# Retention on 64x64 TensorE tiles from batch 2 on, with compact states and paired query loads

## The chip, the cores and the metric

One core of a Trainium2 chip runs the whole program. The metric is the device time in microseconds (us); the times are medians of several executions. Engines: PE is TensorE, DVE VectorE, ACT ScalarE, POOL GpSimd, SP SyncE, which here mainly issues DMAs.

## The reference

Eight batches of eight heads, 576 positions, head size 64. Retention without softmax, then a two-layer perceptron with GELU over all 4608 tokens:

```python
scores = scale * np.matmul(q, k.transpose(0, 1, 3, 2))      # q, k, v: (8, 8, 576, 64)
Dmat = np.where(rel >= 0, gamma[h] ** rel, 0.0)              # rel = i - j, one gamma for each head
attn = np.matmul(scores * Dmat, v)                           # (8, 8, 576, 64)
x = attn.transpose(0, 2, 1, 3).reshape(4608, 512)
h = x @ w_in                                                 # 512 -> 2048
out = gelu_tanh(h) @ w_out                                   # 2048 -> 512, float32
```

## The kernel before

**Chunks.** Each batch is four chunks `c` of 128 positions and a tail of 64. Inside a chunk the product is computed directly and masked; what lies before it comes through a running state of 64x64 for each head. The decay is folded into scale factors that are multiplied onto q and k when they are cast to fp16 (`cast`), so that masks hold only ones and zeros. Heads go in four pairs `p`; `hl` is the head in its pair. A chunk takes, on PE:

- `score`: keys times queries, 64 rows by 128 columns of the array, for each head 128 columns, into two banks `st`, which DVE multiplies by the causal mask `cm` into `ret` (`masks`);
- `past`: the state before the chunk times the queries, on the whole array, with the two states of a pair on the diagonal of a 128x128 block (`tbd`, zeros elsewhere; `tbt` holds the state for the tail);
- `av`: `ret` times values, 128 rows by 64 columns, added into the same bank `xs`;
- `state`: keys times values, added to the running state by `scan` (DVE) and copied into `tbd` by `spread` (ACT, two copies of 64 partitions each).

`put` (ACT) copies `xs` into `xT`, the perceptron's transposed input. The tails of two batches go together (`load_tails`, `cast_tails`, then `score`, `past`, `av` and `put` with a batch number from 100 on). Batches 0 and 1 (`b < NPE`) use another form already: two tokens on a partition, and 64x64 tiles of the array (`score2`, `state2`, `av2`).

**Loads.** `pump` issues the loads on SP in the order of `seq`, as the 16 buffers `ld` come free: batch 0, `w_in` in 16 blocks of 128 rows, `w_out`, batch 1, then the others. A load of a later batch takes 128 positions of all heads, in packets of 256 bytes. Keys and queries are then transposed by two DMAs (`turn_dma`, also on SP).

**Perceptron.** Nine blocks `t` of 512 tokens. In a block, 16 steps of `up` (128x512 products with `w_in`, GELU on ACT into `gT`, sums on DVE by `act_sums`) are followed by 14 half products `prod` with `w_out`; both layers save products by sums of submatrices. The last two blocks (`WIN`) use that for the first layer too.

**Order.** It is written out by hand. `at(t, u, f)` places `f` behind step `u` of block `t`; PE, ACT, DVE and POOL take their instructions in this order. Retention of batch `t + 1` lies in block `t`: scores of chunks 0 and 1 at `s0` (step 9 or 11), their outputs at `o0` (15) with the scores of chunks 2 and 3, whose outputs are at `o1` (24); the tails of `TP` had their scores at `s0` and their outputs at `o0`. In block 1 the steps are 21, 23, 25 and 28. Casts of batch `t + 2` stand at steps 16 to 23 and its transposes behind them.

**Banks.** All eight PSUM banks are handed out by `bank` in the order in which `drop` gave them back, so a new use of a bank waits for its last reader.

Of the kernel before, what the change touches and what calls it, by code (L numbers as in the profile page):

```python
# [20 lines left out]
def kernel(  # L21
# [27 lines left out]
    NT4 = 4  # L49
# [41 lines left out]
    def load(b, key, c):  # L91
        src = SRC[key]
        t = lds()
        if b < NPE:
            g, y = c // 2, c % 2
            nc.sync.dma_start(  # L96
                out=t.rearrange("p (n x) -> p n x", n=4),
                in_=src[b, y::2, 256 * g : 256 * g + 256, :].rearrange("n (p j) d -> p n (j d)", j=2),
            )
        else:  # L100
            nc.sync.dma_start(  # L101
                out=t.rearrange("p (h d) -> p h d", d=D),
                in_=src[b, :, 128 * c : 128 * c + 128, :].rearrange("h s d -> s h d"),
            )
        att[b]["raw"][key, c] = t
# [3 lines left out]
    def load_w_in(g, ct):  # L109
        t = lds()  # L110
        nc.sync.dma_start(out=t, in_=moe_w_in[128 * ct : 128 * ct + 128, 512 * g : 512 * g + 512])
        w_raw["i", g, ct] = t
# [50 lines left out]
    ip = const.tile([128, 4], I32, name="ip")  # L163
    nc.gpsimd.iota(ip[:, 0:2], pattern=[[1, 2]], base=-64, channel_multiplier=2)
    nc.gpsimd.iota(ip[:, 2:4], pattern=[[0, 2]], base=-64, channel_multiplier=1)
# [3 lines left out]
    ps5 = const.tile([128, 8], F32, name="ps5")  # L169
    nc.vector.tensor_copy(out=ps5[:, 0:4], in_=ip)  # L170
    for s, m in ((slice(0, 2), 128.0), (slice(3, 4), 64.0)):
        nc.vector.tensor_scalar(out=ps5[64:128, s], in0=ps5[64:128, s], scalar1=m, scalar2=None, op0=ALU.subtract)
    nc.vector.tensor_scalar(out=ps5[:, 4:8], in0=ps5[:, 0:4], scalar1=-1.0, scalar2=None, op0=ALU.mult)
    lp = const.tile([128, 64], F32, name="lp")
    sc = const.tile([128, 64], F32, name="sc")

    def pairs(x, n):
        return x[:, 16 * n : 16 * n + 16].rearrange("p (n j l) -> p n j l", j=2, l=2)

    lg = lgr.rearrange("p (n l) -> p n l", l=2).unsqueeze(2).to_broadcast([128, 4, 2, 2])  # L180
    for n in range(2):
        pj = ps5[:, 4 * n : 4 * n + 2].unsqueeze(1).unsqueeze(3).to_broadcast([128, 4, 2, 2])
        nc.vector.tensor_tensor(out=pairs(lp, n), in0=lg, in1=pj, op=ALU.mult)
        nc.vector.tensor_tensor(
            out=lp[:, 32 + 16 * n : 48 + 16 * n].rearrange("p (x h) -> p x h", h=8),
            in0=ps5[:, 4 * n + 2 : 4 * n + 4].unsqueeze(2).to_broadcast([128, 2, 8]),
            in1=lgr.unsqueeze(1).to_broadcast([128, 2, 8]), op=ALU.mult,
        )
    lq = lp.rearrange("p (g n x) -> p g n x", g=2, n=2)[:, :, 0]
    nc.vector.tensor_scalar(out=lq, in0=lq, scalar1=math.log(scale), scalar2=None, op0=ALU.add)  # L190
    nc.scalar.activation(out=sc, in_=lp, func=AF.Exp)
    sp = {key: sc[:, 16 * n : 16 * n + 16].rearrange("p (n l) -> p n l", l=2) for n, key in enumerate("qk")}
    sc = sc[:, 32:64].rearrange("p (s h) -> p s h", h=8)
# [7 lines left out]
    cm = const.tile([128, 128], F32, name="cm")  # L201
    tm = const.tile([128, 128], F32, name="tm")
# [11 lines left out]
    def chunk_masks():  # L214
        for m in (cm, tm):
            nc.gpsimd.memset(m, 1.0)
            nc.gpsimd.affine_select(
                out=m, in_=m, compare_op=ALU.is_ge, fill=0.0, base=0, pattern=[[1, 128]], channel_multiplier=-1
            )
        nc.gpsimd.memset(tm[0:64, 64:128], 0.0)  # L220
# [5 lines left out]

    tbt = [const.tile([128, HP, 128], F16, name=f"tbt{i}") for i in range(NT4)]

# [27 lines left out]
    def cast(b, key, c, eng):  # L256
# [8 lines left out]
        elif b < NPE:  # L265
# [7 lines left out]
        else:  # L273
            s0 = {"q": 0, "k": 2}[key] + (b >= PAIR)
# [3 lines left out]
                in1=sc[:, s0].unsqueeze(2).to_broadcast([128, 8, D]),  # L278
# [36 lines left out]

    def tq(b, c, p):
        return att[b]["tt"][:, 1, 8 * (c // 2) + 2 * p + c % 2 if b < NPE else 4 * c + p, :]
# [49 lines left out]
    def av2(b, g):  # L367
        a = att[b]
        for p in range(HP):
            for j in range(2):  # L370
                o = 256 * (p % 2) + 128 * j
                for h, hl in TILES:
                    nc.tensor.matmul(
                        a["xs", 2 * g + h][hv(hl), 128 * p : 128 * p + 128],
# [4 lines left out]
    def score(b, c):  # L379
        st = [bank("st") for _ in range(2)]  # L380
        for p in range(HP):
            for hl in range(2):
                nc.tensor.matmul(  # L383
                    st[hl][:, 128 * p : 128 * p + 128], att[b]["tt"][hv(hl), 0, 4 * c + p, :],
                    tq(b, c, p)[hv(hl)], start=True, stop=True,
                )
        att[b]["st", c] = st

    def masks(b, c):
        for hl, t in enumerate(att[b].pop(("st", c))):  # L390
            r = sb.tile([128, 512], F16, tag="ret", name="ret", bufs=6)
            nc.vector.tensor_tensor(  # L392
                out=r.rearrange("p (n i) -> p n i", i=128), in0=t.rearrange("p (n i) -> p n i", i=128),
                in1=(cm if b < PAIR else tm).unsqueeze(1).to_broadcast([128, 4, 128]), op=ALU.mult,
            )
            drop(t)
            att[b]["ret"][c, hl] = r
# [4 lines left out]
    def state(b, *cs):  # L402
        a = att[b]
        us = bank("us")
        for n, c in enumerate(cs):
            for p in range(HP):
                for hl in range(2):
                    nc.tensor.matmul(
                        us[64 * hl : 64 * hl + 64, 256 * n + 64 * p : 256 * n + 64 * p + 64],
                        a["k"][:, col(c, p, hl)],  # L410
                        a["v"][:, col(c, p, hl)],
                        start=True, stop=True,
                    )
            a["U", c] = (us, n, n == len(cs) - 1)
# [15 lines left out]
    def spread(b, c, cp):  # L430
        w = att[b].pop(("w", c))
        for hl in range(2):
            r = slice(64 * hl, 64 * hl + 64)
            cp(out=(tbd[b % 2][r, c, :, r] if c < NC - 1 else tbt[b % NT4][r, :, r]), in_=w[r])  # L434

    def past(b, c):
        xs = bank("xs")
        att[b]["xs", c] = xs
        if b >= PAIR:
            for n in range(2):  # L440
                for p in range(HP):
                    o = 64 * n
                    nc.tensor.matmul(
                        xs[:, 128 * p + o : 128 * p + o + 64], tbt[(b - PAIR + n) % NT4][:, p, :],
                        tq(b, 0, p)[:, o : o + 64],
                        start=(n == p == 0), stop=True, skip_group_check=True,
                    )
        elif c > 0:
# [6 lines left out]
    def av(b, c):  # L455
        a = att[b]
        for p in range(HP):
            for hl in range(2):
                nc.tensor.matmul(  # L459
                    a["xs", c][64 * hl : 64 * hl + 64, 128 * p : 128 * p + 128],  # L460
                    a["v"][:, col(c, p, hl)],
                    a["ret"][c, hl][:, 128 * p : 128 * p + 128],
                    start=(b < PAIR and c == 0 and p == 0), stop=True, skip_group_check=True,
                )
# [207 lines left out]
    def after(t, m, u):  # L672
# [7 lines left out]
        def send(o, i):  # L680
            if t < B:
# [107 lines left out]
    nc.vector.memset(tbt[0], 0.0)  # L789
# [25 lines left out]
    past(0, 0), past(0, 1)  # L815
# [17 lines left out]
    past(0, 2), past(0, 3)  # L833
# [24 lines left out]
    at(0, -12, lambda: [V.memset(x, 0.0) for x in (tbd[1][:, 1:], *tbt[1:])])  # L858
# [7 lines left out]
    def group(b, g, turns, s, o, own=True, ahead=(), apart=0, late=None):  # L866
# [19 lines left out]
        def second():  # L886
            past(b, 2 * g), past(b, 2 * g + 1), av2(b, g)
# [30 lines left out]
    def scores(t, c, tails=None):  # L918
        b = t + 1
        if b < B:  # L920
            score(b, c), score(b, c + 1)
        if tails is not None:
            score(PAIR + tails, 0)
        if b < B:
            masks(b, c), masks(b, c + 1)
        if tails is not None:
            masks(PAIR + tails, 0)

    def outs(t, c, tails=None, ahead=None):
        b = t + 1  # L930
        work = [(b, c), (b, c + 1)] if b < B else []
# [153 lines left out]
```

## Time and profile before

| | |
|---|---|
| median of three runs | 293.28 us (292.59 to 293.52) |
| profiled execution | 293.76 us, its span 292.0 us |
| granted TensorE clock | 0.996 |
| PE, DVE, ACT, POOL busy | 280.1, 204.1, 169.8, 100.0 us |
| DMA | 139585 packets, 53.95 MB; 118048 of them under 512 bytes |

A timeline line gives the start in the span, the time from the first start to the last end, engine, source line, operation, result and operands, array shape, tile and type, and the count. Matmuls overlap in their pipeline, so a group's time is longer than what it adds to the stream; the step from one group's start to the next one's is what counts.

### The profile page before, as it was taken

To read this page: it belongs to the slowest core of one execution; us is meant where nothing else is said; L and a number is where in the kernel's file an instruction comes from. 1 tells how busy PE (TensorE), PEld (TensorE's weight loads), DVE (VectorE), ACT (ScalarE), POOL (GpSimd) and SP (SyncE) were. 2 spreads that over 40 slices of the span, in tenths; PEclk is the share of its full clock that TensorE was granted. 3 is DMA by queue.
4 is the path that set the end of the run, shared out by engine and by line. 5 is a ranking of instruction groups with operands and counts; after the bars stand their busy time and mean duration, and the time that the engine had idled before them with its cause. 6 is when DMAs were issued, how large, how long until landed. Compare 5 with 4: busy or idle time off the path is not lost.

```text
span 292.0 us, 7383 instructions
## 1 busy us (share of the span) xinstructions
PE 280.1 (96%) x3024; PEld 207.6 (71%) x3024; DVE 204.1 (70%) x409; ACT 169.8 (58%) x321; POOL 100.0 (34%) x128
## 2 busy tenths in 40 slices
PE   6889998999999999999999999999999999999993
PEld 2558877888874687468845884488548887887783
DVE  7796998666864874477548834784489968974863
ACT  5487754987249545964396647664666258507810
POOL 4589779910661175008500730068030000000000
PEclk9999999999999999999999999999999999999998
DMA  6999999989999999999999979997952030003013
GB/s 195 308 382 370 364 293 228 252 213 163 225 192 230 235 206 183 244 235 210 200 267 209 218 147 270 216 190 99 271 95 38 2 144 3 0 21 125 3 36 108
DMA packets 139585, 53.95 MB, mean 185 GB/s; under 512 B 118048, under 2 KB 131360, under 8 KB 139552
## 3 DMA queue, kind: packets, MB, share of 16 engines
q1 hardware_dynamic: 138960, 52.97, 80.4%
q8 instruction: 23, 0.38, 0.6%
q10 hardware_dynamic: 592, 0.52, 0.5%
q14 instruction: 10, 0.08, 0.1%
HBM read 36.70 MB, written 9.44 MB: 158 GB/s over the span
## 4 chain that ended last, share of the span: by engine, by line
PE 66%; SPq 8%; DMA 8%; ACT 5%; POOL 5%; DVE 5%; issue 1%; POOLq 0%; DVEq 0%; ACTq 0%
PE hp L480 18%; PE opB L665 11%; PE opA L665 8%; PE opC L665 7%; SPq L101 5%; DMA ld<-in_moe_w_in_dram 4%; PE hp L501 4%; PE hB L574 3%; SPq L96 3%; ACT gT L486 3%; PE xs L459 2%; POOL w_out_sb L771 2%; PE st L383 2%; DMA ld<-in_v_dram 2%; DMA ld<-in_q_dram 2%; PE hC L574 2%
## 5 line engine op out<-in xcount | busy, mean ns | idle before, releaser
L480 PE MATMUL hp<-xT,w_in_sb 128*128 128x512 f16 x352 | 79.1, 379 | 0.6 <-ACT xT L469 0.3
L486 ACT ACTIVATE gT<-hp 128x512 f16<-128x512 f32 x88 | 50.1, 600 | 22.6 <-PE hp L480 22.0
L480 PEld LDWEIGHTS <-w_in_sb 128*128 128x128 f16 x352 | 34.0, 98 | 39.0 <-issue 1.1
L665 PEld LDWEIGHTS <-gT 128*128 128x128 f16 x576 | 54.9, 98 | 8.9 <-issue 0.9
L665 PEld LDWEIGHTS <-s 128*128 128x128 f16 x432 | 42.2, 98 | 4.9
L642 DVE TENSOR_TENSOR s<-gT 128x512 f16<-128x512 f16 x36 | 15.6, 434 | 31.2 <-ACT gT L486 24.5
L665 PE MATMUL opA<-w_out_sb,gT 128*128 128x256 f16 x288 | 36.0, 273 | 0.6 <-ACT w_out_sb L771 0.4
L392 DVE TENSOR_TENSOR ret<-st,cm 128x512 f16<-128x512 f32 x48 | 30.2, 681 | 3.6 <-PE st L383 3.6
L469 ACT CAST xT<-xs 128x512 f16<-128x512 f32 x36 | 19.2, 590 | 20.4 <-PE xs L459 17.0
L501 PE MATMUL hp<-xT,w_in_sb 128*128 128x256 f16 x256 | 29.9, 273 | 0.9 <-POOL w_in_sb L771 0.5
L275 POOL TENSOR_TENSOR ck<-ld,sc 128x512 f16<-128x512 f32 x24 | 25.0, 1043 | 9.7 <-DMA ld<-in_k_dram 9.7
L501 PEld LDWEIGHTS <-w_in_sb 128*128 128x128 f16 x256 | 24.3, 98 | 5.2 <-POOL w_in_sb L771 2.3
L434 ACT CAST tbd<-ws 64x256 f16<-64x256 f32 x48 | 19.4, 403 | 14.8 <-DVE ws L425 14.2
L275 POOL TENSOR_TENSOR cq<-ld,sc 128x512 f16<-128x512 f32 x24 | 26.1, 1088 | 2.6 <-DMA ld<-in_q_dram 2.1
L665 PE MATMUL opB<-wt,gT 128*128 128x256 f16 x224 | 26.8, 273 | 0.0
L979 POOL COPY gate<-s 128x1 f16<-128x1 f16 x5 | 0.9, 190 | 74.6 <-DVE s L646 74.6
L262 ACT CAST cv<-ld 128x512 f16<-128x512 f32 x24 | 14.2, 618 | 17.2 <-DMA ld<-in_v_dram 17.1
L508 ACT ACTIVATE gT<-hp 128x512 f16<-128x512 f32 x32 | 18.3, 605 | 3.5 <-PE hp L501 3.3
L679 DVE TENSOR_TENSOR k<-k,opB 128x512 f32<-128x512 f32 x17 | 11.7, 686 | 11.7 <-PE opB L665 10.7
L644 DVE TENSOR_TENSOR gT<-gT 128x512 f16<-128x512 f16 x36 | 18.0, 499 | 0.0
L665 PE MATMUL opB<-wt,s 128*128 128x256 f16 x144 | 17.4, 273 | 0.0
L665 PE MATMUL opC<-wt,s 128*128 128x256 f16 x144 | 17.2, 272 | 0.0
(122 smaller groups left out, 406.4 us busy)
## 6 DMA issues: line engine op xcount, KB each, us to landing
ld<-in_q_dram SPq DMA_DIRECT2D x32, 256.0 KB, 5.2
ld<-in_k_dram SPq DMA_DIRECT2D x32, 256.0 KB, 5.1
ld<-in_v_dram SPq DMA_DIRECT2D x32, 256.0 KB, 5.3
out_dram<-ost SPq DMA_DIRECT2D x16, 512.0 KB, 3.9
ld<-in_moe_w_in_dram SPq DMA_DIRECT2D x16, 256.0 KB, 5.7
ld<-in_moe_w_out_dram SPq DMA_DIRECT2D x16, 256.0 KB, 5.6
lt<-in_k_dram SPq DMA_DIRECT2D x8, 128.0 KB, 4.7
lt<-in_q_dram SPq DMA_DIRECT2D x8, 128.0 KB, 4.4
```

Of the source, the lines that this page charges most:

```text
L101: nc.sync.dma_start(out=t.rearrange("p (h d) -> p h d", d=D), in_=src[b, :, 128 * c : 128 * c + 128, :].rearrange("h s d -> s h d"),)
L275: eng.tensor_tensor(out=dst.rearrange("p (h d) -> p h d", d=D), in0=raw.rearrange("p (h d) -> p h d", d=D), in1=sc[:, s0].unsqueeze(2).to_ ...
L392: nc.vector.tensor_tensor(out=r.rearrange("p (n i) -> p n i", i=128), in0=t.rearrange("p (n i) -> p n i", i=128), in1=(cm if b < PAIR else ...
L434: cp(out=(tbd[b % 2][r, c, :, r] if c < NC - 1 else tbt[b % NT4][r, :, r]), in_=w[r])
L469: nc.scalar.copy(out=xT[:, g0 : g0 + 2], in_=xs.rearrange("p (n g t) -> p g n t", n=HP, g=2))
L480: nc.tensor.matmul(hp.rearrange("p (g t) -> p g t", t=TL), w_in_sb[:, ct, 128 * fc : 128 * fc + 128], xT[:, o : o + TB // TL, ct, :], star ...
L486: nc.scalar.activation(out=gT[t][:, fc].rearrange("p i n -> p (i n)"), in_=hp, func=AF.Gelu_apprx_tanh)
L501: nc.tensor.matmul(hps[n][:, 256 * x : 256 * x + 256].rearrange("p (g t) -> p g t", t=TL), w_in_sb[:, ct, 128 * (fs[n] + x) : 128 * (fs[n] ...
L508: nc.scalar.activation(out=gT[t][:, f : f + 2, 2 * u : 2 * u + 2, :].rearrange("p f i n -> p f (i n)"), in_=hp.rearrange("p (f n) -> p f n ...
L642: nc.vector.tensor_tensor(out=s["1"], in0=a21, in1=a22, op=ALU.add)
L644: nc.vector.tensor_tensor(out=a21, in0=a11, in1=a21, op=ALU.subtract)
L665: nc.tensor.matmul(op[tag][:, HD * u : HD * u + HD], lhs(f), rhs[:, f], start=(new and f == 0), stop=(f == NH - 1), skip_group_check=True,)
```

## The change

From batch 2 on and for all tails, every retention product but the first state of batch 2 uses 64x64 tiles: a product of 128 rows is split into two of 64.

- *Scores and values:* the quarter of each 128x128 product that the mask makes zero is left out. One piece has 128 columns, the other 64. Masks cover 384 columns of a bank in place of 512.
- *States* are kept without the zeros of the blocks (`tbc`, `tbt` of 64 columns), one ACT copy each.
- *Queries* are loaded with two tokens on a partition, in packets of 512 bytes, as in batches 0 and 1. Odd chunks of keys and values are loaded in two halves, upper rows first.
- *Output halves:* the heads of odd pairs lie in exchanged halves of `xT` (`hl ^ p % 2`), so odd row blocks of `w_in` are loaded as two exchanged halves. Output rows of blocks 2 to 7 are stored by two DMAs each.
- *Row tiles in turns:* `pack` takes all products of a place together and deals them to the four tiles by columns used so far. In a phase each row tile writes other banks than the other; between phases a matmul of 4 columns into a bank of its own (`TURN`) is issued.
- *Order:* scores of chunks 2 and 3 are packed with the outputs of chunks 0 and 1; tail outputs move from `o0` to `o1`, the third `later` to step 21, the last value cast of batches 4 to 7 from step 23 to 25; block 4 has `s0` at 11.

```diff
-        if b < NPE:
+        if b < NPE or key == "q":
...
+        else:
+            for n in range(2):
+                r0 = 128 * c + 64 - 64 * n
+                nc.sync.dma_start(
+                    out=t[64 * n : 64 * n + 64].rearrange("p (h d) -> p h d", d=D),
+                    in_=src[b, :, r0 : r0 + 64, :].rearrange("h s d -> s h d"),
+                )
...
-        nc.sync.dma_start(out=t, in_=moe_w_in[128 * ct : 128 * ct + 128, 512 * g : 512 * g + 512])
+        for r, n in ((slice(0, 128), 0),) if ct % 2 == 0 else ((slice(0, 64), 64), (slice(64, 128), -64)):
+            rows = slice(128 * ct + r.start + n, 128 * ct + r.stop + n)
+            nc.sync.dma_start(out=t[r], in_=moe_w_in[rows, 512 * g : 512 * g + 512])
...
-    cm = const.tile([128, 128], F32, name="cm")
-    tm = const.tile([128, 128], F32, name="tm")
+    cm = const.tile([128, 192], F32, name="cm")
+    tm = const.tile([128, 64], F32, name="tm")
...
+        two = lambda n: [[1, 2], [2, n // 2]]
+        causal(cm, 128, 0, 64, 64, two(64)), causal(cm, 128, 64, 128, 64, two(128))
+        causal(cm, 64, 0, 128, 0, two(128)), causal(cm, 64, 128, 64, 0, two(64))
+        causal(tm, 128, 0, 64, 64, [[1, 64]]), causal(tm, 64, 0, 64, 0, [[1, 64]])
...
+    def pack(*phases, n=None):
+        opened = set()
+        for phase in phases:
+            if not phase:
+                t = ps.tile([128, 512], F32, tag=f"p{n}", name="turn", bufs=1)
+                nc.tensor.matmul(t[0:64, 0:4], ident[0:64, 0:64], ident[0:64, 0:4], start=True, stop=True)
+                continue
+            todo = {x: deque() for x in TILES}
+            for r, jobs in phase:
+                for x, *job in jobs:
+                    if r in (x[0], None):
+                        todo[x].append(job)
+            free = dict.fromkeys(TILES, 0)
+            while any(todo.values()):
+                x = min((x for x in TILES if todo[x]), key=lambda x: free[x])
+                t, out, lhsT, rhs, cols = todo[x].popleft()
+                k = (id(t), x[1])
+                nc.tensor.matmul(out, lhsT, rhs, start=k not in opened, stop=True, skip_group_check=True)
+                opened.add(k)
+                free[x] += cols
+        if n is not None:
+            spare.append(n)
+
+    TURN = ()
+
+    def piece(o, first):
+        w = 128 if first else 64
+        return o if first else 1 - o, w, 0 if o == 0 else 64 if first else 128
+
+    def score(b, g, x, first=(0, 1)):
...
+        return [
+            ((r, h), st[r], by_two(st[r][hv(h), i + 192 * (p % 2) : i + 192 * (p % 2) + w]),
+             a["tt"][hv(r), 0, 4 * (2 * g + o) + p, hv(h)], tq2(b, 2 * g + o, p, r, w), w)
+            for p in (2 * x, 2 * x + 1) for first in (True, False) for o in range(2)
+            for h, w, i in [piece(o, first)] for r in range(2)
+        ]
...
+        if b >= NPE or c == NC - 1:
+            cp(out=tbt[b % NT4] if c == NC - 1 else tbc[b % 2][:, c], in_=w)
+            return
...
+    def outs(b, g, tails=None, ahead=None, more=False):
+        n = spare.popleft()
+        x, y = outputs(b, g)
+        if more:
+            u, = state(*ahead)
+            s, z = score(b, 1, 0), score(b, 1, 1, (1, 0))
+            pack(
+                [(0, x), (1, y), (0, u), (1, s[:8])], TURN, [(None, s[8:]), (0, s[:8]), (1, z)], TURN,
+                [(0, y), (1, x), (0, z), (1, u)], n=n,
+            )
+        elif tails is not None:
+            t, = outputs_tails(PAIR + tails, 1)
+            if ahead is not None:
+                u, = state(*ahead)
+                pack([(0, t), (1, u)], TURN, [(0, x), (1, y)], TURN, [(0, u), (1, t)], TURN, [(0, y), (1, x)], n=n)
+            else:
+                pack([(1, t)], [(0, x), (1, y)], TURN, TURN, [(0, y), (1, x), (0, t)], n=n)
+        elif ahead is not None:
+            u, v = state(*ahead)
+            pack([(0, u), (1, v)], TURN, [(0, x), (1, y)], TURN, [(0, v), (1, u)], TURN, [(0, y), (1, x)], n=n)
+        else:
+            pack([(0, x), (1, y)], TURN, TURN, [(0, y), (1, x)], n=n)
+        put(b, 2 * g), put(b, 2 * g + 1)
+        if tails is not None:
+            put_tails(PAIR + tails)
...
-        s0, o0, s1, o1 = U2 if t == 1 else (11 if t in (2, 3) else 9, 15, 15, 24)
+        s0, o0, s1, o1 = U2 if t == 1 else (11 if t in (2, 3, 4) else 9, 15, 15, 24)
...
-        t0, ut, go = b - 2, [16, 16, 17, 18, 18, 19, 20, 20, 21, 22, 22, 23], 29
+        t0, ut, go = b - 2, [16, 16, 17, 18, 18, 19, 20, 20, 21, 22, 22, 25], 29
```

In `piece`, `o` is the chunk in its pair of chunks, `first` the piece of 128 columns. In the lists of `outs`, `(0, x)` means the products of list `x` on row tile 0.

## The prediction

> **What bounds the kernel now.** The page comes first: part 1 (busy time) and the PE and DMA rows of part 2 (40 slices of 7.3 us).
>
> ```profile
> PE 280.1 (96%) x3024; PEld 207.6 (71%) x3024; DVE 204.1 (70%) x409; ACT 169.8 (58%) x321; POOL 100.0 (34%) x128
> ...
> PE   6889998999999999999999999999999999999993
> ...
> DMA  6999999989999999999999979997952030003013
> ```
>
> TensorE (PE) works 280 of 292 us, and from the fifth slice on it hardly pauses; no other engine passes 70%. So what the change takes out of PE's own stream counts nearly one for one, unless something else becomes late. The DMA row is full until about 200 us, so loads are the first suspect for being late. The PE timeline of block t=2 shows what retention costs there:
>
> ```profile
> 94.88 0.62 PE L383 MATMUL st<-tt 64*128 64x128 f16 x16
> 95.44 3.63 PE L480 MATMUL hp<-xT,w_in_sb 128*128 128x512 f16 x16
> 98.90 0.39 PE L450 MATMUL xs<-tt,tbd 128*128 128x128 f16 x4
> 99.22 0.64 PE L459 MATMUL xs<-ret,cv 128*64 128x128 f16 x16
> 99.69 0.42 PE L408 MATMUL us<-cv,ck 128*64 128x64 f16 x16
> 100.04 0.62 PE L383 MATMUL st<-tt 64*128 64x128 f16 x16
> 100.59 1.92 PE L665 MATMUL opA<-w_out_sb,gT 128*128 128x256 f16 x16
> ...
> 108.46 0.61 PE L450 MATMUL xs<-tt,tbd 128*128 128x128 f16 x8
> 109.00 0.64 PE L459 MATMUL xs<-ret,cv 128*64 128x128 f16 x16
> 109.47 0.42 PE L408 MATMUL us<-cv,ck 128*64 128x64 f16 x16
> 109.82 1.05 PE L665 MATMUL opA<-w_out_sb,gT 128*128 128x256 f16 x8
> ```
>
> Read start against next start. Sixteen score matmuls (L383) lie between dense work for 0.56 us; the block at 98.90 takes 1.69 us, the one at 108.46 1.36 us. In the recorded starts, a pair of two half-array products is 56 ns apart from the next pair at 128 columns and 28 to 32 ns at 64. Each change of array shape costs 93 to 100 ns over that. Four 64x64 tiles at once occur only in batches 0 and 1:
>
> ```profile
> 53.92 0.45 PE L359 MATMUL us<-cv,ck 64*64 64x64 f16 x32
> 54.20 0.62 PE L332 MATMUL st<-tt 64*64 64x128 f16 x32
> 54.75 2.81 PE L501 MATMUL hp<-xT,w_in_sb 128*128 128x256 f16 x24
> ```
>
> 32 of 64 columns take 0.28 us and 32 of 128 take 0.55 us with the way out. The four of a quartet start 3 to 4 ns apart; quartets follow after 32.2 ns (64 columns) or 55.6 ns (128). These are the prices of everything the change adds. The whole block costs 0.91 us against dense work on both sides, and 8 x 32.2 + 8 x 55.6 ns is 0.70, so entering and leaving costs 0.2 us.
>
> **PE, before.** I take each retention block from batch 2 on as the next dense start, less the previous dense start and that matmul's 109 or 216 ns. By block: t=1 0.64 + 1.29 + 0.64 + 1.35; t=2 0.64 + 1.68 + 1.35; t=3 and t=4 (with tails) 0.86 + 2.14 + 1.35 each; t=5 as t=2; t=6 0.86 + 2.14 + 1.10; t=7 0.42 + 0.66. Sum 25.1 us.
>
> **PE, after.** The built program has 21 blocks on 64x64 tiles with 528 matmuls of 128 columns and 928 of 64: 132 x 55.6 + 232 x 32.2 ns = 14.8 us. Scores and values fall by a quarter of their columns, past states by half, state products keep theirs. Phases that end in a turn wait for the fullest of the four tiles; walking the built order with these spacings adds 1.4 us. The 32 turns (64x64, 4 columns) have no row. From below they cost 4 ns, the gap inside a quartet; from above a shape change, 95 ns. I take 32 ns, the nearest row (the 64-column quartet: weights of the same size must load for each), in all 0.9 us. The Trainium skill, TensorEngine Tiling (Array Packing), Instruction Overhead, gives a short matmul about 60 cycles; at the 2.4 GHz that its page TensorE: Matmul & The Clock Gate gives, an estimate is 25 ns a turn and 0.7 us in all, and no run here shows it.
>
> Entering and leaving is 21 x 0.2 = 4.2 us. In the built order each later turn of a block also waits for the turn before it, whose result takes about as long as a 64-column matmul, 193 ns. Where 16 short matmuls lie between (four times) some 90 ns stay uncovered, where two turns follow each other (twice) some 200 ns: 0.75 us. Sum 14.8 + 1.4 + 0.9 + 4.2 + 0.75 = 22.1 us, so PE gains 3.0 us. With turns of 4 ns and those waits free it is 4.6 us, with turns of 95 ns 1.1 us.
>
> **Waits on PE.** At t=1, step 23, the two state banks are the last two score banks. DVE drains four masks in 2.48 us (74.04 to 76.5); at three quarters of the columns I take 0.53 each, to 76.1, while PE comes to them near 75.8. What is queued behind is all of PE: +0.3 us. At the later blocks the banks are older by four dense steps (3.5 us). Against this, one wait should go:
>
> ```profile
> 113.06 0.62 ACT L262 CAST cv<-ld 128x512 f16<-128x512 f32 x1 [3.63 <-DMA ld<-in_v_dram]
> ...
> 114.70 10.52 PE L480 MATMUL hp<-xT,w_in_sb 128*128 128x512 f16 x48 [0.34 <-ACT xT L469]
> ```
>
> ACT sits in a cast that waits for a load, the output copy (`put`) is behind it, and PE idles 0.34 us. The last value cast moves from step 23 to 25, behind that copy: -0.3 us.
>
> **DVE, ACT, POOL.** Masks shrink from 512 to 384 columns, and the 64 half-height state copies (`spread`, 403 ns each) become 38; with ACT at 58% and DVE at 70% this is worth nothing on the path. Two half copies for the last tails cost some 0.4 us of an ACT that waits then. `chunk_masks` has four more selects on POOL (0.3 us each, less the removed memset): about +1.0 us ahead of batch 2's casts. Its cover is a wait:
>
> ```profile
> 60.01 1.13 POOL L275 TENSOR_TENSOR cq<-ld,sc 128x512 f16<-128x512 f32 x1 [1.91 <-DMA ld<-in_q_dram]
> ```
>
> If this cover went, the 1.0 us would reach the transposes. Start-up constants gain one DVE operation and lose memsets: 0, bounds 0.2 us either way.
>
> **Loads and stores.** A 256-byte packet took 22.2 ns on average, one of 512 bytes 30.6. A load of 256 KB is then 1.42 or 0.98 us of 16 engines; 24 query loads save 10.6 us of a DMA system that is busy 80% of 292. Each odd key or value load becomes two halves: SP issues of the halved tail loads took 0.63 us each, whole ones at least 0.57, query loads of 512 bytes 0.37. So a batch's issues go from 12 x 0.6 to 4 x 0.38 + 4 x 0.6 + 8 x 0.63, 7.2 to 9.0 us. They now leave SP over 15.6 us (93.18 to 108.77), at the pace of the DMA, so this hides. Output stores of blocks 2 to 7 are cut in two: 2 x 0.4 us on SP ahead of the next loads, hidden the same way. The eight extra `w_in` issues fall where loads leave every 0.7 us for 0.33 us of issue; fewer bytes are then in flight, 0 to 0.5 us, I take 0.2. The tails' products move from step 15 to 24; at t=6 the transpose on SP that waits for them (7.8 us now) waits some 10 us more, with only stores behind it that come later still and its reader at 244.
>
> The narrowest place is the transposed batch:
>
> ```profile
> L308 SPq DMA_TRANSPOSE tt<-cq x1: 3251/3251/3251, 67.5 to 67.5; - x1
> ...
> DMA to landing us min/median/max: 5.6/7.0/8.4
> ```
>
> The query transpose issued at 67.47 landed 5.6 us later, at 73.1; PE reads it at 73.54. For t=2 the slack is 93.9 to 94.88; from t=3 on 3 us and more.
>
> **Sum.** -3.0 + 0.3 - 0.3 + 0.2 = -2.8 us. The profiled execution took 293.76 us (span 292.0, 1.7 around it), the median 293.28. From the median: 290.5 us.
>
> **Rivals.**
> *Turns are dear (slower).* If a turn drains the array, the next phase starts only when the last result is written: 216 ns, the length of one 128-column matmul. 14.8 + 1.4 + 4.2 + 32 x 0.216 = 27.3 us, 2.2 more than before, 295.7 with the rest. It decides from about 140 ns a turn on. For it: a turn exists to keep two row tiles out of one bank, and some turns do wait for another. Against it: most wait only for a turn long past, and even a shape change costs 95 ns. Chance 0.10.
>
> *Issue limit (slower).* Batches 0 and 1 never run more than 64 small matmuls in a row; the new blocks run up to 115, with 398 beyond their 64th. Were those single file at 28 ns instead of about 10, it is +7.2 us, 297.7; the gain is gone from 7 ns more each. The Trainium skill, TensorE: Matmul & The Clock Gate, Wait — 56ns, not 53.3ns?, states that starts are never closer than about 25 ns; the trace disagrees (3 to 4 ns inside a quartet). Chance 0.04.
>
> *The feed takes the gain (same).* If loads are bound by SP's issues and not by bytes, 16 issues at today's 1.2 us make 19.2 us instead of 15.6; the transposes for t=2 come 3.6 us later against 1.0 us of slack, +2.6 us: 293.1. Against it: DMA over full in that stretch, and fewer packets. Chance 0.10.
>
> *A larger gain.* Turns at 4 ns, no waits among them, no bank wait: -4.6 - 0.3 + 0.2 gives 288.6. Chance 0.11. My forecast has 0.65.
>
> **Numbers.** The range runs from 288.3 (just past the larger gain) to 293.5 (just past the feed). About 0.3%, 0.9 us, is what a measurement of this kernel can tell from no change. Faster: 0.65 + 0.11 = 0.76; same: 0.10; slower: 0.10 + 0.04 = 0.14.
>
> **What would show it.** In the profile after: blocks at t=2 of about 0.56, 1.45 and 1.25 us between dense matmuls instead of 0.64, 1.68 and 1.35; the quartets 56 and 32 ns apart to the end of a block; first matmuls after a turn some 32 ns late; PE busy 277 us. It is wrong if turns leave gaps over 150 ns, or if score matmuls wait for a transpose.

## The result, and the profile after

The changed kernel takes 302.99 us (302.43 to 304.08, four runs), the kernel before 292.99 us beside it: a ratio of 1.0345, 95% interval 1.0309 to 1.038. The forecast was 290.5 us, with 293.5 us at the top of its range. Here and below, medians and ranges take in all executions; ratios leave out those more than 1.5% above the fastest of the same kernel. The profiled execution has a span of 301.4 us, 9.4 more than before.

From the page after, part 1 and three rows of part 2 (40 slices of 7.5 us; PEclk is the clock granted to TensorE, in tenths of full speed, DMA the busy share of the DMA engines):

```profile
PE 280.4 (93%) x3784; PEld 204.8 (68%) x3784; DVE 192.1 (64%) x406; ACT 158.1 (52%) x296; POOL 100.4 (33%) x131
...
PE   6869798999999999999899989999989899999992
...
PEclk9979799999999999999999999999999999999998
...
DMA  7998999999997999999899997999995061005013
```

PE's busy time did not fall, though the work on it did: the PE row has new dips, and in the third and fifth slices the granted clock fell too. What PE waited for is in the view of its waits (total us, times, longest):

```profile
PE hp L619 <- POOL w_in_sb L894: 4.2, 6, 1.0
PE us L419 <- ACT cv L278: 2.8, 2, 1.4
...
PE st L419 <- DMA tt<-cq: 0.9, 1, 0.9
PE opB L783 <- DVE k L797: 0.8, 1, 0.8
...
PE st L419 <- DMA ett<-e: 0.6, 2, 0.4
```

Before, the first of these was 0.5 us and the second and third did not exist. All but the fourth, a wait for VectorE in the perceptron, lead to loads. Two places carry the loss.

**The start.** The SP timelines of the stretch that loads `w_in`, of before and of after (start, time from the first to the last issue):

```profile
9.85 11.33 SPq L111 DMA_DIRECT2D ld<-in_moe_w_in_dram  x16
```

```profile
9.38 17.59 SPq L120 DMA_DIRECT2D ld<-in_moe_w_in_dram  x24
```

The stretch is 6.3 us longer, and the first product with `w_out` comes that much later, at 39.27 us after 33.04 (PE timeline after):

```profile
30.52 0.28 PE L619 MATMUL hp<-xT,w_in_sb 128*128 128x256 f16 x1 [0.37 <-POOL w_in_sb L894]
31.60 0.28 PE L619 MATMUL hp<-xT,w_in_sb 128*128 128x256 f16 x1 [0.80 <-POOL w_in_sb L894]
32.67 6.75 PE L619 MATMUL hp<-xT,w_in_sb 128*128 128x256 f16 x45 [0.79 <-POOL w_in_sb L894]
39.27 1.91 PE L783 MATMUL opA<-w_out_sb,gT 128*128 128x256 f16 x16
```

**The feed.** In blocks 3 and 4 the pack of outputs at step 24 holds state products, and those wait for the last value cast, which waits for its load (PE, then ACT, both after):

```profile
145.78 0.22 PE L419 MATMUL us<-cv,ck 64*64 64x64 f16 x2 [1.42 <-ACT cv L278]
```

```profile
145.11 0.62 ACT L278 CAST cv<-ld 128x512 f16<-128x512 f32 x1 [4.47 <-DMA ld<-in_v_dram]
```

**PE's own work** got shorter, as forecast. Where nothing waits, the retention blocks of t=2 lie between dense matmuls for 0.56, 1.36 and 1.24 us, those with tails for 0.68 to 1.39 us. Start against next start in the timeline of t=2:

```profile
101.35 0.54 PE L419 MATMUL st<-tt 64*64 64x128 f16 x32
101.83 3.63 PE L598 MATMUL hp<-xT,w_in_sb 128*128 128x512 f16 x16
...
114.78 0.17 PE L407 MATMUL turn<-ident 64*64 64x4 f16 x1
114.78 0.30 PE L419 MATMUL xs<-tt,tbd 64*64 64x128 f16 x8
```

A turn delays what follows by almost nothing: 28 of the 32 starts behind a turn come within 7 ns. The wait lies ahead of some turns: six of them start 152 to 285 ns after the matmul before them, the others within 32 ns.

So the question for the runs was which part of the loads costs the time, and whether the gain on PE is there without it.

### The profile page after: what moved, and what is told of

The parts are those of the page before. It is cut to its first block, busy times and chain, and to the rows that moved or that the text cites. A ratio compares the mean times of both kernels' runs of the same rounds, so it can differ in the third digit from the quotient of the medians.

```text
span 301.4 us, 8960 instructions
## 1 busy us (share of the span) xinstructions
PE 280.4 (93%) x3784; PEld 204.8 (68%) x3784; DVE 192.1 (64%) x406; ACT 158.1 (52%) x296; POOL 100.4 (33%) x131
## 5 line engine op out<-in xcount | busy, mean ns | idle before, releaser
L604 ACT ACTIVATE gT<-hp 128x512 f16<-128x512 f32 x88 | 51.6, 597 | 20.1 <-PE hp L598 19.8
L598 PEld LDWEIGHTS <-w_in_sb 128*128 128x128 f16 x352 | 34.0, 98 | 38.2 <-issue 0.4
L760 DVE TENSOR_TENSOR s<-gT 128x512 f16<-128x512 f16 x36 | 18.2, 505 | 37.7 <-ACT gT L604 25.9
L283 POOL TENSOR_TENSOR cq<-ld,sc 128x512 f16<-128x512 f32 x31 | 34.0, 1101 | 10.1 <-DMA ld<-in_q_dram 10.1
L619 PE MATMUL hp<-xT,w_in_sb 128*128 128x256 f16 x256 | 32.4, 285 | 4.3 <-POOL w_in_sb L894 4.2
L619 PEld LDWEIGHTS <-w_in_sb 128*128 128x128 f16 x256 | 25.2, 102 | 10.1 <-POOL w_in_sb L894 6.2
L445 DVE TENSOR_TENSOR ret<-st,cm 128x384 f16<-128x384 f32 x48 | 23.8, 547 | 7.7 <-PE st L419 7.7
L587 ACT CAST xT<-xs 128x512 f16<-128x512 f32 x32 | 17.2, 588 | 15.2 <-PE xs L419 11.0
L626 ACT ACTIVATE gT<-hp 128x512 f16<-128x512 f32 x32 | 18.3, 599 | 9.9 <-PE hp L619 9.8
L783 PE MATMUL opB<-wt,s 128*128 128x256 f16 x144 | 17.4, 273 | 0.0
L783 PE MATMUL opC<-wt,s 128*128 128x256 f16 x144 | 17.2, 273 | 0.0
L797 DVE TENSOR_TENSOR k<-k,opB 128x512 f32<-128x512 f32 x17 | 11.6, 685 | 8.2 <-PE opB L783 8.2
L762 DVE TENSOR_TENSOR gT<-gT 128x512 f16<-128x512 f16 x36 | 16.7, 464 | 0.0
L761 DVE TENSOR_TENSOR s<-s,gT 128x512 f16<-128x512 f16 x36 | 15.3, 425 | 1.2
```

What stands on the lines that cost most here:

```text
L283: eng.tensor_tensor(out=a[key][:, 1024 * (c // 2) : 1024 * (c // 2) + 1024].rearrange("p (n l d) -> p l n d", l=2, d=D)[:, y], in0=raw.rea ...
L445: nc.vector.tensor_tensor(out=r[:, 0:384].rearrange("p (n i) -> p n i", n=2), in0=t[:, 0:384].rearrange("p (n i) -> p n i", n=2), in1=cm.u ...
L587: nc.scalar.copy(out=xT[:, g0 : g0 + 2], in_=xs.rearrange("p (n g t) -> p g n t", n=HP, g=2))
L598: nc.tensor.matmul(hp.rearrange("p (g t) -> p g t", t=TL), w_in_sb[:, ct, 128 * fc : 128 * fc + 128], xT[:, o : o + TB // TL, ct, :], star ...
L604: nc.scalar.activation(out=gT[t][:, fc].rearrange("p i n -> p (i n)"), in_=hp, func=AF.Gelu_apprx_tanh)
L619: nc.tensor.matmul(hps[n][:, 256 * x : 256 * x + 256].rearrange("p (g t) -> p g t", t=TL), w_in_sb[:, ct, 128 * (fs[n] + x) : 128 * (fs[n] ...
```

## The experiments

Each kernel was timed beside the kernel before on the same chip (its median there 293.02 to 293.73 us). The theory: loads in halves cost both places. The rivals: the number of issues, other new DMAs (stores in two), or the retention work itself. Where loads of the changed kernel are made whole, the exchange of the halves of odd blocks is left out: the work and its order are the same, the output is another one, until the last section of this part makes the exchange in another place.

### `w_in` whole

```diff
-        for r, n in ((slice(0, 128), 0),) if ct % 2 == 0 else ((slice(0, 64), 64), (slice(64, 128), -64)):
+        for r, n in ((slice(0, 128), 0),):
```

> The changed kernel with every w_in block loaded whole, by one DMA; the odd blocks' halves are then not exchanged, so the numbers of the odd pairs are computed with the wrong rows, the work and its order are the same. Theory A (half loads): w_in took 17.6 us of SP issue (9.38 to 27.0) instead of 11.3, and PE came to the first w_out product at 39.27 instead of 33.04; whole loads give back 5 to 6 us, so 297 to 298 us, first opA near 33.5. Theory B (other start-up edits: constants, masks, the copies of batches 0 and 1): the time stays at 302 to 303.

Measured: 296.45 us (ratio 1.0117, 1.0068 to 1.0166), 6.5 us less than the changed kernel. That is a little under the expected 297 to 298 us. Its waits for `w_in` fell to 0.7 us and its first product with `w_out` came at 33.5 us; those of the feed stayed (2.4 us for `cv`, 1.1 us for `tt`). The start is explained by these loads.

### Keys and values whole

```diff
-        elif c % 2 == 0:
+        elif c >= 0:
```

> The changed kernel with odd key and value chunks of batches 2 to 7 loaded whole, by one DMA, not exchanged (the mask then falls on wrong rows; work and order are the same); w_in stays in halves. Theory A (half loads feed too late): the waits of PE for value casts (0.4, 1.4, 1.4 us) and for transposes (0.4, 0.9, 0.2 us), some 5.6 us with their restarts, go: 297 to 299 us. Theory B (PE's own new blocks are dear): stays at 302 to 303, since the blocks without waits keep their length.

Measured: 301.75 us (1.0293, 1.0261 to 1.0325), only 1.2 us less, and not the expected 297 to 299 us. All waits of the feed are gone, but those for `w_in` grew (6.1 us after 4.2), and a new one is there:

```profile
PE hp L619 <- POOL w_in_sb L894: 6.1, 7, 2.0
PE xs L529 <- DVE ret L364: 2.9, 2, 2.7
```

### All loads whole

Both edits together.

> Both together: w_in and all keys and values by whole loads, nothing exchanged (wrong rows in odd blocks and chunks, same work). Theory A: both losses go and what is left is what the prediction counted for PE, 3.0 to 3.5 us: 289 to 291 us, faster than before. Theory B: 297 us or more. Output stores stay cut in two; if they matter, the result lies between, at 292 to 294.

Measured: 295.6 us (1.0087, 1.0055 to 1.012). A miss: with every half gone it is still slower than before. The start is back at 33 us and the feed no longer waits; the new wait is the same. The PE, DVE and POOL timelines around it, one after the other:

```profile
60.95 0.38 PE L529 MATMUL xs<-tt,tbd 128*128 128x128 f16 x4 [2.67 <-DVE ret L364]
```

```profile
55.12 0.42 DVE L506 TENSOR_TENSOR vs<-us,ws 128x256 f32<-128x256 f32 x1 [2.60 <-PE us L382]
55.58 4.71 DVE L509 TENSOR_TENSOR ws<-vs,gt 128x256 f32<-128x256 f32 x1
60.22 2.47 DVE L364 TENSOR_TENSOR ret<-st,pm 128x512 f16<-128x512 f32 x4
```

```profile
55.96 1.03 POOL L291 TENSOR_TENSOR ck<-ld,sc 128x512 f16<-128x512 f32 x1
56.97 1.04 POOL L283 TENSOR_TENSOR cq<-ld,sc 128x512 f16<-128x512 f32 x1
57.97 1.03 POOL L291 TENSOR_TENSOR ck<-ld,sc 128x512 f16<-128x512 f32 x1
58.97 1.04 POOL L283 TENSOR_TENSOR cq<-ld,sc 128x512 f16<-128x512 f32 x1
```

A multiplication in batch 1's state update (`scan`), 0.43 us at most other places, is recorded with 4.71 us. It is not waiting for a semaphore: it has begun and does not finish until POOL's row of casts ends at 60.01. Behind it on DVE are the masks of batch 1, behind it on ACT the copy of the state and the evictions of `gT`. It has two operands in SBUF; the addition before it, with one in PSUM, took its usual time. The Trainium skill, SBUF — State Buffer, Who interferes with whom, says that a VectorE instruction with two SBUF inputs and a GpSimd instruction that reads SBUF exclude each other. That made a theory that could be tested.

### The sum left in PSUM, for batch 1

To the kernel with all loads whole:

```diff
-            s = sb.tile([128, HP, 64], F32, tag="vs", name="vs", bufs=1)
+            s = uc if b == 1 else sb.tile([128, HP, 64], F32, tag="vs", name="vs", bufs=1)
```

> The kernel with all loads whole (295.6 us), and in the state update of batch 1 alone the sum of state and product is left in its PSUM bank, so that the multiplication behind it reads one operand from SBUF instead of two. As there, odd w_in, k and v rows are not exchanged, so the retention part of the output is another one. Theory (VectorE's multiplication with two SBUF operands, 4.71 us instead of 0.43 us at 55.6 us, stands still for as long as GpSimd casts without a gap, to 60.0 us, and holds the masks behind it and ScalarE's copy of the state): the multiplication takes 0.4 to 0.6 us there, PE's 2.9 us of waits for masks at 61 us and the slow stretch after them go, 291 to 292.5 us. Rival (the masks or the copy wait for something else that is late, a load or a bank): the multiplication is short but PE still waits at 61 us, 294.5 to 296 us.

Measured: 289.28 us (288.93 to 290.67; ratio 0.9876, 0.9842 to 0.991), 6.3 us less for one operand moved and below the expected 291 to 292.5 us. POOL casts as densely as before, and DVE's multiplication reads `us` in PSUM:

```profile
54.09 0.43 DVE L506 TENSOR_TENSOR us<-us,ws 128x256 f32<-128x256 f32 x1 [2.67 <-PE us L382]
54.56 0.42 DVE L509 TENSOR_TENSOR ws<-us,gt 128x256 f32<-128x256 f32 x1
54.90 2.47 DVE L364 TENSOR_TENSOR ret<-st,pm 128x512 f16<-128x512 f32 x4
```

No wait of PE for masks is left in the view of waits. The gain exceeds the 2.9 us of waits: the multiplication held ACT's evictions too, and PE ran slower behind the pause (80 products of 256 columns after it took 9.60 us there, 8.91 here; the granted clock was 0.86 from 61 to 73 us there, 1.00 here). From the last products before the pause to the next product with `w_out` it is 17.30 us there and 12.50 here, so 4.8 us of the gain lie in this place. Another 1.1 us lie ahead of it, where PE waits 0.7 us for `w_out` in that profile and not in this one; the multiplication does not explain these.

### The sum left in PSUM, for all batches

The same line without the condition on `b`.

> As the one with the sum kept in PSUM for batch 1, but for all batches. The multiplications that take 1.0 to 1.2 us in other batches (8 of them, 0.8 us too long each) become 0.45 us. Theory: they stand before the state copies but lie beside dense matmuls, so the time is that of the kernel with batch 1 alone within 0.5 us. Rival (they sit on a path: copies of the states come earlier, outputs wait less): 0.5 to 2 us less. Other rival (the PSUM bank of the state products is held 0.5 us longer and PE waits for banks): 0.5 to 2 us more.

Measured: 289.97 us (0.9897, 0.9856 to 0.9938), the same within the scatter. No multiplication of `scan` is long any more; the others (1.0 to 1.2 us, one cast of POOL each) had cost nothing.

### The same edit in the kernel before

> The kernel before with the sum of the state update of batch 1 left in PSUM, nothing else. There the multiplication takes 1.3 us at 54.6 us and the masks' wait of PE is 0.2 us. Theory (the standing multiplication is a matter of the whole-load changed kernel, where GpSimd's casts have no gap): 292.6 to 293.3 us, no change that can be measured. Rival (part of the gain of the changed kernel with whole loads is this edit alone, and the kernel before would have it too): 290.5 to 292 us.

Measured: 293.38 us beside 293.34 (1.0002, 0.998 to 1.0024). In the kernel before nothing hangs on it; the edit alone is no gain.

### The kernel before with `w_in` in halves

```diff
-        nc.sync.dma_start(out=t, in_=moe_w_in[128 * ct : 128 * ct + 128, 512 * g : 512 * g + 512])
+        for r in (slice(0, 128),) if ct % 2 == 0 else (slice(0, 64), slice(64, 128)):
+            rows = slice(128 * ct + r.start, 128 * ct + r.stop)
+            nc.sync.dma_start(out=t[r], in_=moe_w_in[rows, 512 * g : 512 * g + 512])
```

> The kernel before, with only the odd w_in blocks loaded in two halves of 64 partitions, in their own rows (nothing else changes, the numbers are right). Theory A: 5 to 6 us slower than before, 298 to 299 us, with 2 KB packets of 120 to 130 ns during w_in instead of 88. Theory B: as before, 293 us.

Measured: 299.68 us (1.0239, 1.0191 to 1.0288), 6.7 us more than before and a little above the expected time: the whole loss of the start, without any other part of the change.

### Cut by columns, and by every other row

Two more cuts of the same blocks in the kernel before, into as many issues: `t[:, 0:256]` and `t[:, 256:512]`, and `t[0::2]` and `t[1::2]`.

> The kernel before; the odd blocks of w_in are still loaded in two issues each, but cut by columns: both issues reach all 128 partitions, with rows of 1 KB instead of 2 KB. As many issues (24) as with the halves by rows. If it is the number of issues that cost 6.7 us in the kernel before with halves (18.1 us for 24 issues, as in the kernel after), this costs the same: some 299 to 300 us, first opA near 39 us. If it is that a transfer reaches only 64 partitions, the issues take 24 x 0.45 us = 11 to 13 us, the packets of 1 KB about half of the 88 ns of 2 KB, first opA stays at 33 to 34 us, and the time is 293 to 294.5 us.

> The kernel before; the odd blocks of w_in are loaded in two issues of 64 rows each, as with the halves, but one takes the even and one the odd rows and partitions, so that each issue reaches partitions from 0 to 127. As many issues, bytes for each issue and row lengths (2 KB) as with the halves (299.7 us). If what costs is the number of issues or the 128 KB of each, this is as slow as with the halves: 298.5 to 301 us, packets of 2 KB at 125 ns. If it is that one issue lies in one half of the partitions: the packets come back to 88 to 100 ns and the time to 293 to 295 us. Between: both have a part, as the blocks cut by columns (296.5 us) suggest.

Measured: by columns 296.52 us (1.0119, 1.008 to 1.0158), by every other row 297.88 us (1.0154, 1.0124 to 1.0184). Neither extreme holds: the ratios give 3.5 and 4.5 us, between 0 and the halves' 7.0. The windows from 15 to 25 us of the kernel before, the changed kernel, then the kernel before with halves, every other row and columns (stretch and its length, busy time of PE, PEld, DVE, ACT and POOL; last three columns: granted clock, DMA share, GB/s):

```profile
15.00:25.00 10.00, 9.04 (x160) 6.74 (x160) 7.76 (x18) 7.93 (x17) 8.42 (x13) 1.00 1.03 367
```

```profile
15.00:25.00 10.00, 7.66 (x140) 5.57 (x137) 4.90 (x11) 5.45 (x13) 6.35 (x10) 0.83 0.89 239
```

```profile
15.00:25.00 10.00, 7.56 (x135) 5.28 (x136) 6.25 (x14) 5.76 (x13) 5.50 (x9) 0.83 0.99 243
```

```profile
15.00:25.00 10.00, 7.91 (x150) 5.86 (x151) 6.46 (x16) 6.88 (x15) 6.36 (x11) 1.00 0.77 245
```

```profile
15.00:25.00 10.00, 6.86 (x135) 4.52 (x133) 7.24 (x16) 6.26 (x14) 6.71 (x11) 0.95 0.88 269
```

The rate fell to between 239 and 269 GB/s in all four, but the DMA engines are full in one of them alone. The issues themselves say more. SP's records of the `w_in` issues, of the kernel before, the changed kernel, every other row and columns (shortest, median and longest in ns, start of the first and the last):

```profile
L111 SPq DMA_DIRECT2D ld<-in_moe_w_in_dram x16: 327/382/1068, 9.8 to 20.8; - x16
```

```profile
L120 SPq DMA_DIRECT2D ld<-in_moe_w_in_dram x24: 465/540/1233, 9.4 to 26.4; - x24
```

```profile
L113 SPq DMA_DIRECT2D ld<-in_moe_w_in_dram x24: 471/536/1254, 9.5 to 25.7; - x24
```

```profile
L112 SPq DMA_DIRECT2D ld<-in_moe_w_in_dram x24: 327/404/1507, 10.7 to 25.3; - x24
```

Before, SP is at these issues for 7.6 of 11.3 us and waits in between. With halves it is at them for 14.5 of 17.4 us, with every other row for 14.5 of 16.9, by columns for 11.6 of 15.0: 24 issues in place of 16, and those of the cuts by rows longer each. The time of the issues by rows is the same whether the DMA engines are full (0.99) or not (0.77), so a full DMA is not what makes them long. The stretch of the issues grows by 6.1, 5.5 and 3.7 us and the kernel by 7.0, 4.5 and 3.5. So most of the loss is time of the queue that issues, by number and by length of the issues. That is read from the traces; no run moved the issues to another queue, which would test it.

Halves cost 2.5 us more than every other row. With them the packets of 2 KB are slower (126 ns from 18 to 21 us in the changed kernel, 128 in the kernel before with halves, 103 with every other row, 89 before), and the clock fell to 0.83, in the changed kernel too, where it stayed at 1.00 with every other row. The runs do not separate these two. On the packets the Trainium skill, SBUF — State Buffer, "Can I just issue two DMAs to hit both halves?", says that only a transfer over all 128 partitions reaches all ports; the difference of halves and every other row agrees with it.

### The kernel before with keys and values in halves

> The kernel before; the odd k and v chunks of batches 2 to 7 are loaded as two transfers of 64 partitions each, rows where they were. Its retention work and its turns are those of before. Theory (the halves use up the slack of the batch loads): the later v casts come late, PE waits for state products 1 to 4 us in all, 294 to 297 us. Rival (the slack of the kernel before covers it; the waits of the kernel after need also its shorter blocks and its states in the same pack as the outputs): within 0.3% of 293.0 us, and no wait of PE for a cast above 0.3 us from batch 2 on.

Measured: 296.43 us (294.85 to 299.43; 1.0106, 1.0037 to 1.0174). With the whole retention work of before, the halves cost about 3 us, with a wide scatter. The time is in the range of the theory, but no state product waits for a cast. The profiled execution, one of the faster ones, shows another form: ACT waits 4.11 us for a value load, the output copy is queued behind that cast, and PE behind the copy.

```profile
114.59 0.62 ACT L268 CAST cv<-ld 128x512 f16<-128x512 f32 x1 [4.11 <-DMA ld<-in_v_dram]
```

```profile
116.24 4.04 PE L486 MATMUL hp<-xT,w_in_sb 128*128 128x512 f16 x18 [2.11 <-ACT xT L475]
```

The 0.34 us that PE idles at this place in the kernel before became 2.11.

### The exchange made by the casts

To the kernel with whole loads and the sum in PSUM: every odd block is cast by two instructions of 64 partitions, each writing the other half.

```diff
+        turned = [(hv(1 - x), hv(x)) for x in range(2)] if swap else [(slice(0, 128),) * 2]
...
+            for o, i in turned:
+                eng.tensor_tensor(
+                    out=dst[o].rearrange("p (h d) -> p h d", d=D),
...
+        if kind == "i" and i[1] % 2:
+            nc.scalar.copy(out=dst[0:64], in_=src[64:128])
+            nc.gpsimd.tensor_copy(out=dst[64:128], in_=src[0:64])
```

> The whole change with whole loads: the exchange of the two partition halves of odd blocks is made by the casts, two instructions of 64 partitions each that write the other half (k on GpSimd; v on the engine that had it; w_in one half on ScalarE and one on GpSimd), and in the state update of batch 1 the sum stays in PSUM. It computes the reference. Theory (the halves of the loads and the standing multiplication were all that kept the time from the forecast; an exchange at the cast costs 2 x 1.04 us of GpSimd and some 1.2 us for v per batch beside work that hides them): 289 to 291 us. Rival (the second cast of each odd block delays the last k and v casts by some 2 us and the w_in casts at the start by up to 5 us, as the loads in halves did): PE waits for w_in, cv or tt again, 292 to 296 us.

With the ScalarE half of `w_in` on VectorE instead:

> As the kernel that exchanges the halves at the cast, but the ScalarE part of the w_in exchange (8 casts of 64 partitions) is on VectorE. If ScalarE's queue (its evictions of gT take 0.60 of each 0.87 us from 21 to 33 us) is what the exchange slows, this is 0.5 to 2 us faster than with ScalarE; if VectorE stands still while GpSimd casts, its masks and sums come late and it is as slow or slower by 0.5 to 2 us. Where the exchange is hidden both ways: the same within 0.5 us.

Measured: 299.52 us (1.02, 1.0154 to 1.0245) and 295.2 us (1.0013, 0.9981 to 1.0045; 293.7 us by the ratio). The first is slower than theory and rival said; the second is faster than the first, as its first case said, but by more than 2 us. In the first, PE waits 3.1 us for `xT` and 2.7 us for `w_in`, in the second 3.5 us for `w_in`: the 16 casts stand together in the program, so that on an engine with other work the evictions and state updates queue behind casts that still wait for their loads, or the first casts behind those.

The last version puts the casts of `w_in` where their data lands: the first four after the state copy of chunk 1, the next four around the output copies of chunks 2 and 3, the others at `at(0, n - NF)` for n from 2 to 8.

> As the kernel that exchanges the halves at the cast (ScalarE takes one half of each odd block of w_in, GpSimd the other), but the casts of w_in stand in the program where their data lands: those of the first group ahead of the score products, those of the second around the evictions of the outputs, those of the last two between the pairs of gT evictions. Theory (in the other kernel PE's 5.8 us of waits for w_in and for the evictions xT came from casts that waited for their loads at the head of ScalarE's queue): no wait of PE for w_in or xT above 0.7 us, first opA by 33.5 us, 289.5 to 291.5 us. Rival (the extra casts themselves, 0.43 us on ScalarE beside evictions of 0.60 in each 0.87 us and 0.68 us on GpSimd, are too many): first opA at 34 to 36 us, 292 to 295 us.

Measured: 290.63 us (289.64 to 292.02), ratio 0.9902 (0.9875 to 0.9928) to the kernel before at 293.73. The time is in the expected range. The two signs that were to go with it are not there: PE's waits are not all below 0.7 us, and the first product with `w_out` comes at 35.9 us, where 33.5 was expected and 34 to 36 was the rival's mark. Four rows of PE's waits and one of its timeline, from the profiled execution, the slowest of the six runs:

```profile
PE tr L315 <- DVE ck L286: 1.6, 1, 1.6
PE hp L622 <- ACT w_in_sb L898: 0.9, 1, 0.9
PE hp L622 <- POOL w_in_sb L901: 0.8, 2, 0.4
PE hp L622 <- POOL w_in_sb L899: 0.8, 2, 0.4
```

```profile
35.92 1.91 PE L786 MATMUL opA<-w_out_sb,gT 128*128 128x256 f16 x16
```

Of these 35.9 us, 1.1 lie ahead of the first issue of `w_in`, which is at 11.1 us here and at 10.0 in the profile with whole loads and the sum in PSUM; the other 1.7 us go with the casts of `w_in`. So the start still pays for the exchange, as the rival said, but less than the 292 us and more it expected; none of the feed is left. This is the change with what it meant to do and without its divided loads, and it beats both kernels, the one before by about 1%.

## Why the prediction was wrong

- **PE's work: right, a little too small.** Forecast 22.1 us for the retention blocks from t=1 on, measured 21.6 in the kernel with whole loads, where nothing waits among them: a gain of 3.5 us, where 3.0 was forecast. PE is busy 276.6 us there, forecast 277. The blocks of t=2 were to be 0.56, 1.45 and 1.25 us and are 0.56, 1.36 and 1.24.
- **Turns: near the lower bound.** Of 32, 28 delay the next start by 0 to 7 ns; 32 ns was assumed (which makes 1.0 us for 32 turns, not the 0.9 of the sum). The waits of turns for turns, put at 0.75 us, are there: the six late starts make some 1.0 us, an estimate from their 152 to 285 ns less the 3 to 32 ns ahead of the others. So the sign of gaps over 150 ns is there too, but from a wait that the sum had as a term. *Turns are dear* falls, and so does *Issue limit*: blocks of 112 and more products take 1.39 us without slowing down.
- **"The eight extra `w_in` issues ... 0 to 0.5 us, I take 0.2": the first step that failed.** They cost 6.5 us (changed kernel against the one with `w_in` whole) and 6.7 us in the kernel before. The step gave each half the 0.33 us of issue of a whole load and found room for it in 0.7 us. But the issues took 0.54 us at the median, halves and the whole loads among them, and 24 of them kept SP for 14.5 us where 16 had taken 7.6; the stretch grew from 11.3 to 17.6 us, and the rate from 15 to 25 us fell from 367 to 239 GB/s. The prediction had a nearer row: for the halves of keys and values it took 0.63 us, from the loads of the tails. One whole load of 0.33 and two halves of 0.63 us are 1.6 us for two blocks that used to leave in 1.4, an estimate of some 1.5 us for the eight pairs and already above the bound of 0.5. In a stretch where PE waits for `w_in`, as it did there already for 0.5 us, what comes later goes straight to the end. That these loads cost the time is shown by the runs; that it is by the time of their issue is read from the traces.
- **"So this hides": the second.** Key and value loads in halves cost 7.2 us: 296.45 us with `w_in` whole, 289.28 with all whole and the multiplication out of the way (two edits; in the first of these kernels the multiplication took 1.00 us, so little of it is there). In the kernel before they cost about 3 us. The step again set issue time (9.0 us) against 15.6 us of room. The issues of a batch take 15.0 to 17.2 us in the changed kernel and 12.8 to 15.0 with all loads whole, some 2 us more. The slack was taken as that of SP; the value casts had none, as the wait in ACT's line at 113.06 said, which the step read as a gain.
- **The rival *The feed takes the gain*** had the mechanism: more issues, later loads, waits for casts and a transpose; and one of the prediction's signs of being wrong came true, score products that wait 0.9 us for a transpose. But its 16 issues of 1.2 us are 0.9 to 1.0 us each, it had less than half the price (2.6 us), named the transposes of t=2 where values and the transpose of t=6 (0.9 us) came late, gave it 0.10, and knew nothing of the start.
- **Query loads, masks, selects, stores, start constants:** taken as hidden. The kernel with whole loads has them all and runs at 289.28 us, so nothing of size is left for them.
- **Bank wait +0.3, value cast -0.3:** the first is not in the view of waits; the second is gone at its place, but PE waits 0.2 us for `xT` at the end of block 1, where it did not before. Both are too small to matter.
- **Not foreseen:** the two-operand multiplication. It is in neither kernel of the comparison at this length (before 1.32 us, changed 0.68), and came only when whole loads kept POOL's casts without a gap. It hid the repair of the feed.

The forecast of 290.5 us was for a kernel whose loads cost nothing, and near that it holds: 289.28 us with whole loads, 290.63 us with the exchange paid in casts. That the last lies so close is partly luck, since PE gained 0.5 us more than forecast and the exchange in the casts cost about 1 us that the forecast did not have (0.8 by the ratios, 1.4 by the medians). Put back one after the other, the halves of keys and values add 7.2 us and those of `w_in` 6.5; these are the differences of the measured times and so add up to 302.99 by themselves.

## What to carry to other kernels

A load that is cut in two is not two half loads: price each issue by its recorded time in the form that it will have (0.54 us at the median here, where whole loads took 0.38), see whether the queue that issues still has room, and ask who waits at the end of it. An exchange of rows is cheaper in the cast that must be made anyway, if each cast stands in the program where its data lands. When a repair does not pay, look for an instruction that is longer than its kind before giving up the theory: the next stall may be hidden by the first.

## What the runs showed of the hardware

- Cutting half of the 256 KB loads into two of 128 KB took the rate from 367 to between 239 and 269 GB/s, with the DMA engines busy for 0.77 to 0.99. The median issue on SP grew from 382 ns to between 526 and 540 where the cut was by rows, the whole loads among them too, and to 404 by columns.
- Packets of 2 KB took 126 to 128 ns when each of the two loads lay in one half of the partitions, 103 when each had every other row, 89 when all loads were whole (18 to 21 us).
- A VectorE multiplication with two SBUF operands stood for 4.71 us beside four GpSimd casts that followed each other directly, in two kernels alike. In other places it got through after one cast (1.0 to 1.2 us). What decides this at the end of a cast no run shows.
- Matmuls of 64 rows and 4 columns between phases delayed the next start by 0 to 7 ns in 28 of 32 places; six of them started late themselves, by 152 to 285 ns.
- The granted clock of a stretch with pauses fell to 0.83 with halves and 0.95 by columns (15 to 25 us), and to 0.86 behind the standing multiplication; with every other row, where PE paused too, it stayed at 1.00. Where it falls it adds to the loss: in the first 39 us of the changed kernel, at a mean clock of 0.91, PE was busy 30.9 us for 386 recorded matmuls; before, 388 took 28.3 us.
